# Taps' factors laid out channel by channel, and phases read across by ScalarE

## The chip, the cores and the metric

The kernel runs on one core of a Trainium2 chip. The metric is device time in microseconds, the median of several runs of the same kernel. The engines are TensorE (PE, with its weight loads shown as PEld), VectorE (DVE), ScalarE (ACT), GpSimd (POOL) and SyncE (SP, whose queue issues most DMAs). Each engine works through its own instructions in the order in which they were issued.

## The reference

Two branches over 2048 positions and 512 channels are mixed by a gate per position:

```python
dt = exp(log_dt)                                   # 512 channels
P  = exp(dt * (A_re + i A_im) * l)                 # channels x 128 states x 2048 positions
K  = einsum("dn,dnl,dn->dl", C, P, dt * B).real    # taps: 512 channels x 2048
a  = causal_convolution(u, K) + u * Dskip          # by FFT over 4096 points
b  = gelu(x @ w1 + b1) @ w2 + b2                   # 512 -> 1792 -> 512, x = u
g  = sigmoid((u * gate_w).sum(-1))
out = g * a + (1 - g) * b
```

## The kernel before

The work has two stages. The first, `front`, makes the taps K, runs the dense branch b, and does the first step of the signal's transform. The second, `conv`, finishes the convolution: second transform step of taps and signal, product, inverse transform, mix with the gate and output.

**The order.** `front` does not issue instructions as it goes. Its streams `dense`, `taps`, `signal` and `early` add tasks to a plan, each with an engine, a duration that the planner goes by (`mm(1.83, ...)`, `act(3.14, ...)`, for VectorE worked out from an element count by `vec`), a due time from the table `DUES`, and the tiles that it reads and writes. The planner plays the tasks through on paper and so fixes one order for every engine; the chip then follows that order. Work that waits on an engine holds up everything behind it on that engine.

**The taps.** The 512 channels are handled in 4 units of 128 (`prepare`, `coefficients`), each cut into 4 groups of `CW` = 32 channels, 16 groups in all. A position is split into a low part of 64 values and a high part of 32 values, so that a group's taps are, per channel, a product of two complex factors over the 128 states (the partitions): 32 high samples in `x` (tile `xc`, two copies in the space of `den`) and 64 low samples in `y` (one copy). Per group the steps are

- `phases` (VectorE, L703 and L695): integer phases `ph` by doubling, 33 samples x 32 channels, samples outside, channels inside.
- `waves` (ScalarE, L711 to L713): the absolute value, the sine and the cosine of the phases into `tt`, one copy in the space of `loft`.
- `begin` (ScalarE, L721): copies the first 4 samples of the high factor from `x4` into `xc`.
- `powers` (VectorE): three doublings from 4 to 32 samples by `cmul` (L594 to L597), which multiplies by a coefficient per channel from `zz`, through the scratch tiles `xt_` and `xv_`.
- `magnitudes` (GpSimd L740, VectorE L752 and five times L750): the 64 magnitudes `e`, which is `y[:, 1]`, by doubling from both ends.
- `rotate` (VectorE L763, L770, L774): turns magnitudes and sines into real and imaginary parts of `y`.
- `contract` (TensorE L788): for each channel, a matmul over the 128 states of the 32 high samples (weights, `x`) and the 64 low samples (moving, `y`), real and imaginary part, into one PSUM bank `pks`. Four channels at a time lie in the array's four column tiles. The trace shows two MATMULs for each fp32 product, so 128 for a group. VectorE then adds the skip term (L804), ScalarE copies the bank (L807), and after every second group the first transform step follows (`first_stage`, L489), whose results ScalarE copies (L815) and SyncE stores to `tk_d` in DRAM (L830) after each unit.

In the kernel before, all these tiles have the samples outside and the channels inside: one channel's samples lie 32 values (128 bytes) apart.

**The dense branch.** `hidden` (L985 to L987) multiplies in three parts of high and low halves into `ph` banks of PSUM, ScalarE applies the gelu (L1002) and casts the high half (L1005, `hh`), VectorE takes the difference (L1012, `hl`), and `output` (L1028 to L1031) multiplies by w2.

**The second stage.** `conv` begins with the taps reloaded from `tk_d` (tiles `tk` and `t`) and their transform (L1218), which is also where the chain of the first stage ends.

Of the kernel before, what the change touches and what calls it, by code (L numbers as in the profile page):

```python
# [17 lines left out]
P = 128  # L18
# [12 lines left out]
CW = 32  # L31
# [10 lines left out]
D_KA = 27.96  # L42
# [104 lines left out]
TWO_PI = 2.0 * PI  # L147
TURN = 2.0**32
# [201 lines left out]
def gated_mix(  # L350
# [18 lines left out]
    nc = tc.nc  # L369
# [33 lines left out]
    def front(pool, psum, keep, attic, loft, den, pr):  # L403

        pl = Plan()

        def tiles(n, shape, nm, dtype=F32, space=pool):
            return [space.tile(shape, dtype, name=f"{nm}{k}") for k in range(n)]

        def vec(n, fn, due, reads=(), writes=(), fast=1):  # L410

            return pl.add("DVE", 0.07 + n / 960.0 / fast, fn, due, reads, writes)

        def act(hold, fn, due, reads=(), writes=(), table=None):

            return pl.add("ACT", hold, fn, due, reads, writes, table)
# [20 lines left out]
        xc = [den[:, k : k + 4].rearrange("p k d -> p (k d)").rearrange("p (a b c) -> p a b c", a=2, c=CW) for k in (0, 4)]  # L437
        xt_, xv_ = (loft[:, k * 1024 : k * 1024 + 1024].rearrange("p (a b c) -> p a b c", a=2, c=CW) for k in range(2))
# [37 lines left out]
        step = [0]  # L476
# [108 lines left out]
            )  # L585
            vec(UW, lambda: v.tensor_copy(dtb, pus[1][:, 0:UW]), -190, [("pu", 1)], ["dtb"])

        def cmul(due, dst, a, br, bi, n, t, v, ka, kb, kd, kt, kv):

            w = a.shape[-1]  # L590
            br = br.unsqueeze(1).unsqueeze(1).to_broadcast([P, 2, n, w])
            bi = bi.unsqueeze(1).unsqueeze(1).to_broadcast([P, 2, n, w])
            vv, m = nc.vector, n * w
            vec(2 * m, lambda: vv.tensor_mul(t, a, br), due, [ka, *kb], [kt])  # L594
            vec(2 * m, lambda: vv.tensor_mul(v, a, bi), due, [ka, *kb], [kv])  # L595
            vec(m, lambda: vv.tensor_sub(dst[:, 0], t[:, 0], v[:, 1]), due, [kt, kv], [kd])
            vec(m, lambda: vv.tensor_add(dst[:, 1], t[:, 1], v[:, 0]), due, [kt, kv], [kd])  # L597
# [110 lines left out]

        def waves(t):
            def sines():  # L710
                nc.scalar.activation(tt[:, 0], ph, AF.Abs)  # L711
                nc.scalar.activation(tt[:, 1], ph, AF.Sin, scale=TWO_PI / TURN)
                nc.scalar.activation(tt[:, 0], tt[:, 0], AF.Sin, bias=half_pi, scale=-TWO_PI / TURN)  # L713

            act(3.14, sines, t + D_KA, ["ph"], ["tt"], "sin")

        def begin(c, k, t):

            cs = slice(c * CW, (c + 1) * CW)
            act(  # L720
                0.31, lambda: nc.scalar.copy(xc[k][:, :, 0:4], x4[:, :, :, cs]), t + D_KA,  # L721
                ["x4"], [("xc", k)],
            )
# [12 lines left out]

        def magnitudes(u, c, t):

            cs = slice(c * CW, (c + 1) * CW)
            pl.add("POOL", 0.1, lambda: nc.gpsimd.memset(e[:, 63], 1.0), t, [], ["y1"])  # L740

            def both(lo, step, n):

                a = e[:, lo : lo + n].copy()
                return bass.AP(a.tensor, a.offset, [a.ap[0], [step * CW, 2], *a.ap[1:]])

            def double(k):
                n = 1 << k
                an = ea[u % 2][:, k, cs].unsqueeze(1).unsqueeze(1).to_broadcast([P, 2, n, CW])
                nc.vector.tensor_mul(both(n, 64 - 3 * n, n), both(0, 64 - n, n), an)  # L750

            vec(CW, lambda: nc.vector.tensor_copy(e[:, 0], ea[u % 2][:, 5, cs]), t, [("ea", u % 2)], ["y1"])  # L752
            for k in range(5):
                vec(2 * CW << k, lambda k=k: double(k), t, [("ea", u % 2)], ["y1"])

        def rotate(t):

            v = nc.vector
            cc = tt[:, 0, 0:32]
            cc = bass.AP(cc.tensor, cc.offset, [cc.ap[0], [CW, 2], *cc.ap[1:]])  # L760

            def real():
                v.tensor_mul(  # L763
                    y[:, 0].rearrange("p (a b) c -> p a b c", a=2),
                    e.rearrange("p (a b) c -> p a b c", a=2),
                    cc,
                )
# [6 lines left out]
            vec(32 * CW, lambda: v.tensor_mul(e[:, 32:64], e[:, 32:64], tt[:, 1, 1:33]), t, ["tt"], ["y1"])  # L774

        pair = []

        def contract(u, c, k, t):
            g = u * NCH + c
            q = 0  # L780
            x = xc[k]

            def products(g0):
                for gg in range(g0, g0 + 4):
                    for r in range(2):
                        for j in range(4):
                            ch = j * 8 + gg
                            nc.tensor.matmul(  # L788
                                pks[q][32 * j : 32 * j + 32, :, gg],
                                x[:, r, :, ch],  # L790
                                y[:, r, :, ch],
                                start=(r == 0),
                                stop=(r == 1),
                                skip_group_check=True,
                            )
# [678 lines left out]
```

## Time and profile before

| what | value |
|---|---|
| median of 3 runs | 508.39 us (507.99 to 508.75) |
| span of the profiled execution | 505.5 us, 12181 instructions |
| TensorE clock granted, mean | 0.996 |
| busy over the span: PE, DVE, ACT, POOL | 495.2, 429.2, 365.0, 38.3 us |
| the sixteen contractions | L788, 2048 matmuls, the first at 71.6 us, the last at 376.3 us |

The profile carries the span of the profiled execution alone, from its first to its last instruction; the times of the runs take in what lies around it. In a row of instructions, the form on the right of an arrow is what is read, on the left what is written, as partitions x elements. "Busy" and "mean ns" follow, then the idle time of the engine in front of it with what ended it. In a row of a stretch of time stand its length and, for PE, PEld, DVE, ACT and POOL, the busy time with the number of instructions, then the granted TensorE clock, the share of the DMA engines, and GB/s. In a row of a waits view stand the total in us, the number of times, and the longest. In the timeline and the chain stand start and duration in us.

### The profile page before, as it was taken

The numbers are of one execution on the slowest core, as the hardware profiler recorded it, in microseconds if no ns is written. First come the engines' busy times: TensorE is split into PE (matmuls) and PEld (weight loads), VectorE is DVE, ScalarE is ACT, GpSimd is POOL, SyncE is SP. The second block draws the span as 40 slices with busy tenths as digits, with TensorE's granted clock in tenths as the row PEclk, the third lists the DMA queues.
The fourth block names the chain that finished last, engine by engine and source line by source line (L and its number), as shares of the span: only waits on it lengthen the run. The fifth ranks groups of instructions, "written<-read, shape, count | busy, mean of one in ns | idle before, by whom it ended". The sixth has DMA issues, their size and how long they took to land.

```text
span 505.5 us, 12181 instructions
## 1 busy us (share of the span) xinstructions
PE 495.2 (98%) x4802; PEld 379.0 (75%) x4802; DVE 429.2 (85%) x817; ACT 365.0 (72%) x632; POOL 38.3 (8%) x78
## 2 busy tenths in 40 slices
PE   8999999999999999999999999999999999999994
PEld 7898888898989889888988888998989522222551
DVE  4977999999999999999999999999940197877455
ACT  6999997899997789997767998636834465565310
POOL 2000000000000000001010020110100100231000
PEclk9999999999999999999999999999999999999998
DMA  8978686531858622855987244950477999989897
GB/s 286 350 280 278 188 243 213 161 126 43 280 138 246 200 73 72 254 168 116 232 217 241 75 64 128 186 100 3 154 219 169 259 389 389 338 305 391 294 344 299
DMA packets 81569, 107.56 MB, mean 213 GB/s; under 512 B 39284, under 2 KB 43784, under 8 KB 80968
## 3 DMA queue, kind: packets, MB, share of 16 engines
q1 hardware_dynamic: 74792, 82.80, 51.8%
q0 software_dynamic: 6016, 20.70, 15.4%
q10 hardware_dynamic: 704, 3.28, 1.8%
q8 instruction: 38, 0.62, 0.5%
q14 instruction: 19, 0.16, 0.1%
HBM read 61.14 MB, written 45.62 MB: 211 GB/s over the span
## 4 chain that ended last, share of the span: by engine, by line
PE 93%; DMA 2%; SPq 1%; DVE 1%; issue 1%; ACT 0%; POOL 0%; DVEq 0%; POOLq 0%
PE pk L788 12%; PE ph L985 10%; PE acc L1028 10%; PE ph L987 10%; PE ph L986 10%; PE acc L1029 9%; PE acc L1031 9%; PE p2k L1218 5%; PE p2u L1218 5%; PE pa L1257 3%; PE ph L489 3%; PE pb L1373 2%; DMA tk<-tk_d 1%; SPq L830 1%; DMA tk_d<-sk 1%; PE acc L1101 1%
## 5 line engine op out<-in xcount | busy, mean ns | idle before, releaser
L985 PE MATMUL ph<-xh,wh 128*128 128x256 f32 x448 | 127.5, 285 | 0.0
L987 PE MATMUL ph<-xh,wl 128*128 128x256 f32 x448 | 126.8, 283 | 0.0
L986 PE MATMUL ph<-xlo,wh 128*128 128x256 f32 x448 | 126.7, 283 | 0.0
L985 PEld LDWEIGHTS ph<-xh,wh 128*128 128x128 f32 x448 | 85.2, 190 | 6.9 <-issue 4.0
L986 PEld LDWEIGHTS ph<-xlo,wh 128*128 128x128 f32 x448 | 85.1, 190 | 2.1
L987 PEld LDWEIGHTS ph<-xh,wl 128*128 128x128 f32 x448 | 85.2, 190 | 0.0
L1028 PE MATMUL acc<-wh,hh 128*128 128x512 f32 x208 | 84.3, 405 | 0.0
L1029 PE MATMUL acc<-wl,hh 128*128 128x512 f32 x208 | 81.7, 393 | 0.0
L1031 PE MATMUL acc<-wh,hl 128*128 128x512 f32 x208 | 81.4, 391 | 0.0
L1002 ACT ACTIVATE ph<-ph,b1t 128x256 f32<-128x256 f32 x112 | 50.5, 451 | 25.0 <-PE ph L987 23.2
L788 PE MATMUL pk<-y,den 128*32 128x64 f32 x2048 | 61.4, 290 | 0.0
L788 PEld LDWEIGHTS pk<-y,den 128*32 128x32 f32 x2048 | 57.2, 136 | 2.6 <-issue 0.7
L1012 DVE TENSOR_TENSOR hl<-ph,hh 128x512 fp32r<-128x512 f32 (+1 forms) x62 | 38.2, 618 | 18.3 <-ACT hh L1005 10.8
L1028 PEld LDWEIGHTS acc<-wh,hh 128*128 128x128 f32 x208 | 39.1, 188 | 19.4 <-issue 8.8
L750 DVE TENSOR_TENSOR y<-y,ea 128x64 f32<-128x64 f32 (+4 forms) x80 | 45.3, 566 | 0.8 <-POOL y L740 0.3
L1031 PEld LDWEIGHTS acc<-wh,hl 128*128 128x128 f32 x208 | 39.1, 188 | 8.8
L1029 PEld LDWEIGHTS acc<-wl,hh 128*128 128x128 f32 x208 | 39.1, 188 | 6.1
L1226 ACT COPY k<-p2k 128x512 f32<-128x512 f32 x32 | 18.6, 586 | 27.2 <-issue 11.3
L594 DVE TENSOR_TENSOR loft<-den,zz 128x256 f32<-128x256 f32 (+2 forms) x48 | 37.2, 774 | 0.2
L595 DVE TENSOR_TENSOR loft<-den,zz 128x256 f32<-128x256 f32 (+2 forms) x48 | 37.2, 775 | 0.1
L763 DVE TENSOR_TENSOR y<-y,loft 128x2048 f32<-128x2048 f32 x16 | 36.6, 2286 | 0.4 <-ACT loft L713 0.2
L1005 ACT CAST hh<-ph 128x512 fp32r<-128x512 f32 (+1 forms) x62 | 33.0, 533 | 4.3 <-PE acc L1029 2.4
(197 smaller groups left out, 873.3 us busy)
## 6 DMA issues: line engine op xcount, KB each, us to landing
tk_d<-sk SPq DMA_DIRECT2D x32, 256.0 KB, 5.3
t_d<-sa SPq DMA_DIRECT2D x32, 256.0 KB, 5.1
tu_d<-attic SPq DMA_DIRECT2D x40, 128.0 KB, 3.5
attic<-in_xt_dram SPq DMA_DIRECT2D x16, 256.0 KB, 4.3
attic<-in_xs_dram SPq DMA_DIRECT2D x16, 256.0 KB, 5.0
xl_d<-xlo SPq DMA_DIRECT2D x8, 512.0 KB, 5.9
xh_d<-xh SPq DMA_DIRECT2D x8, 512.0 KB, 3.9
out_dram<-io SPq DMA_DIRECT2D x16, 256.0 KB, 3.1
```

The lines of the kernel that those rows point to most:

```text
L594: vec(2 * m, lambda: vv.tensor_mul(t, a, br), due, [ka, *kb], [kt])
L750: nc.vector.tensor_mul(both(n, 64 - 3 * n, n), both(0, 64 - n, n), an)
L788: nc.tensor.matmul(pks[q][32 * j : 32 * j + 32, :, gg], x[:, r, :, ch], y[:, r, :, ch], start=(r == 0), stop=(r == 1), skip_group_check=True,)
L985: nc.tensor.matmul(p, h, xh[xk][:, d], start=(d == 0), stop=False)
L986: nc.tensor.matmul(p, h, xlo[xk][:, d], start=False, stop=False)
L987: nc.tensor.matmul(p, lo, xh[xk][:, d], start=False, stop=(d == 3))
L1002: nc.scalar.activation(phs[q][:, n], phs[q][:, n], AF.Gelu_apprx_tanh, bias=b1t[:, f : f + 1])
L1012: nc.vector.tensor_sub(lo, phs[q][:, 0:nf], hi.bitcast(F32))
L1028: nc.tensor.matmul(a, h, wh[1][w], start=start, stop=False, skip_group_check=seeded)
L1029: nc.tensor.matmul(a, h, wl[1][w], start=False, stop=False, skip_group_check=seeded)
L1031: nc.tensor.matmul(a, l, wh[1][w], start=False, stop=stop, skip_group_check=seeded)
L1218: nc.tensor.matmul(out[64 * i : 64 * i + 64], w, x, start=True, stop=True)
```

## The change

All tiles of the two factors get channels outside and samples inside, so that one channel's samples are neighbours: `y` becomes `[P, 2, CW, 64]`, `xc` `[P, 2, CW, 32]`, `xt_` and `xv_` alike, `tt` `[P, 2, CW, 33]`. The phases `ph` stay as they were; the first two passes of `waves` read them across and write `tt` in the new order. `begin` reads `x4` across. `cmul` gets a form `inner`, in which the coefficient of a channel is repeated along the samples (the innermost dimension); `coefficients` keeps the old form. `magnitudes` and `rotate` do the same operations on the same counts in the new order. The matmuls of `contract` take `x[:, r, ch]` and `y[:, r, ch]`, 32 and 64 neighbours. The durations handed to the planner are unchanged.

```diff
-        y = pool.tile([P, 2, 64, CW], F32, name="y")
-        xc = [... .rearrange("p (a b c) -> p a b c", a=2, c=CW) for k in (0, 4)]
-        xt_, xv_ = (... .rearrange("p (a b c) -> p a b c", a=2, c=CW) for k in range(2))
-        tt = loft[:, 2048:4160].rearrange("p (a b c) -> p a b c", a=2, c=CW)
+        y = pool.tile([P, 2, CW, 64], F32, name="y")
+        xc = [... .rearrange("p (a c b) -> p a c b", a=2, c=CW) for k in (0, 4)]
+        xt_, xv_ = (... .rearrange("p (a c b) -> p a c b", a=2, c=CW) for k in range(2))
+        tt = loft[:, 2048:4160].rearrange("p (a c b) -> p a c b", a=2, c=CW)
...
-        def cmul(due, dst, a, br, bi, n, t, v, ka, kb, kd, kt, kv):
+        def cmul(due, dst, a, br, bi, n, t, v, ka, kb, kd, kt, kv, inner=False):
-            w = a.shape[-1]
-            br = br.unsqueeze(1).unsqueeze(1).to_broadcast([P, 2, n, w])
-            bi = bi.unsqueeze(1).unsqueeze(1).to_broadcast([P, 2, n, w])
+            w = CW if inner else a.shape[-1]
+            shape, at = ([P, 2, w, n], 3) if inner else ([P, 2, n, w], 1)
+            br = br.unsqueeze(1).unsqueeze(at).to_broadcast(shape)
+            bi = bi.unsqueeze(1).unsqueeze(at).to_broadcast(shape)
...
         def waves(t):
             def sines():
-                nc.scalar.activation(tt[:, 0], ph, AF.Abs)
-                nc.scalar.activation(tt[:, 1], ph, AF.Sin, scale=TWO_PI / TURN)
+                turned = ph.rearrange("p b c -> p c b")
+                nc.scalar.activation(tt[:, 0], turned, AF.Abs)
+                nc.scalar.activation(tt[:, 1], turned, AF.Sin, scale=TWO_PI / TURN)
                 nc.scalar.activation(tt[:, 0], tt[:, 0], AF.Sin, bias=half_pi, scale=-TWO_PI / TURN)
...
-                0.31, lambda: nc.scalar.copy(xc[k][:, :, 0:4], x4[:, :, :, cs]), t + D_KA,
+                0.31, lambda: nc.scalar.copy(xc[k][:, :, :, 0:4], x4[:, :, :, cs].rearrange("p a b c -> p a c b")), t + D_KA,
...
-                    t, x[:, :, n : 2 * n], x[:, :, 0:n], zz[:, 0, i, cs], zz[:, 1, i, cs], n,
-                    xt_[:, :, 0:n], xv_[:, :, 0:n], ("xc", k), ["zz"], ("xc", k), "xt", "xv",
+                    t, x[:, :, :, n : 2 * n], x[:, :, :, 0:n], zz[:, 0, i, cs], zz[:, 1, i, cs], n,
+                    xt_[:, :, :, 0:n], xv_[:, :, :, 0:n], ("xc", k), ["zz"], ("xc", k), "xt", "xv", True,
...
-            pl.add("POOL", 0.1, lambda: nc.gpsimd.memset(e[:, 63], 1.0), t, [], ["y1"])
+            pl.add("POOL", 0.1, lambda: nc.gpsimd.memset(e[:, :, 63], 1.0), t, [], ["y1"])
...
-                an = ea[u % 2][:, k, cs].unsqueeze(1).unsqueeze(1).to_broadcast([P, 2, n, CW])
+                an = ea[u % 2][:, k, cs].unsqueeze(1).unsqueeze(3).to_broadcast([P, 2, CW, n])
                 nc.vector.tensor_mul(both(n, 64 - 3 * n, n), both(0, 64 - n, n), an)
-            vec(CW, lambda: nc.vector.tensor_copy(e[:, 0], ea[u % 2][:, 5, cs]), t, ...)
+            vec(CW, lambda: nc.vector.tensor_copy(e[:, :, 0], ea[u % 2][:, 5, cs]), t, ...)
...
-                    y[:, 0].rearrange("p (a b) c -> p a b c", a=2),
-                    e.rearrange("p (a b) c -> p a b c", a=2),
+                    y[:, 0].rearrange("p c (a b) -> p a c b", a=2),
+                    e.rearrange("p c (a b) -> p a c b", a=2),
                     cc,
...
-                v.scalar_tensor_tensor(e[:, 0:32], e[:, 0:32], -1.0, tt[:, 1, 0:32], ALU.mult, ALU.mult)
+                v.scalar_tensor_tensor(e[:, :, 0:32], e[:, :, 0:32], -1.0, tt[:, 1, :, 0:32], ALU.mult, ALU.mult)
...
-                                x[:, r, :, ch],
-                                y[:, r, :, ch],
+                                x[:, r, ch],
+                                y[:, r, ch],
```

More of the change, by code (lines that the diff above doesn't have):

```diff
@@ L435, in front @@
         sk = pool.tile([P, 64, 2, 4, 8], F32, name="sk")
-        y = pool.tile([P, 2, 64, CW], F32, name="y")
-        xc = [den[:, k : k + 4].rearrange("p k d -> p (k d)").rearrange("p (a b c) -> p a b c", a=2, c=CW) for k in (0, 4)]
-        xt_, xv_ = (loft[:, k * 1024 : k * 1024 + 1024].rearrange("p (a b c) -> p a b c", a=2, c=CW) for k in range(2))
-        tt = loft[:, 2048:4160].rearrange("p (a b c) -> p a b c", a=2, c=CW)
+        y = pool.tile([P, 2, CW, 64], F32, name="y")
+        xc = [den[:, k : k + 4].rearrange("p k d -> p (k d)").rearrange("p (a c b) -> p a c b", a=2, c=CW) for k in (0, 4)]
+        xt_, xv_ = (loft[:, k * 1024 : k * 1024 + 1024].rearrange("p (a c b) -> p a c b", a=2, c=CW) for k in range(2))
+        tt = loft[:, 2048:4160].rearrange("p (a c b) -> p a c b", a=2, c=CW)
         ph = pool.tile([P, 33, CW], I32, name="phase")
@@ L739, in magnitudes @@
             cs = slice(c * CW, (c + 1) * CW)
-            pl.add("POOL", 0.1, lambda: nc.gpsimd.memset(e[:, 63], 1.0), t, [], ["y1"])
+            pl.add("POOL", 0.1, lambda: nc.gpsimd.memset(e[:, :, 63], 1.0), t, [], ["y1"])
             def both(lo, step, n):
-                a = e[:, lo : lo + n].copy()
-                return bass.AP(a.tensor, a.offset, [a.ap[0], [step * CW, 2], *a.ap[1:]])
+                a = e[:, :, lo : lo + n].copy()
+                return bass.AP(a.tensor, a.offset, [a.ap[0], [step, 2], *a.ap[1:]])
             def double(k):
                 n = 1 << k
-                an = ea[u % 2][:, k, cs].unsqueeze(1).unsqueeze(1).to_broadcast([P, 2, n, CW])
+                an = ea[u % 2][:, k, cs].unsqueeze(1).unsqueeze(3).to_broadcast([P, 2, CW, n])
                 nc.vector.tensor_mul(both(n, 64 - 3 * n, n), both(0, 64 - n, n), an)
-            vec(CW, lambda: nc.vector.tensor_copy(e[:, 0], ea[u % 2][:, 5, cs]), t, [("ea", u % 2)], ["y1"])
+            vec(CW, lambda: nc.vector.tensor_copy(e[:, :, 0], ea[u % 2][:, 5, cs]), t, [("ea", u % 2)], ["y1"])
             for k in range(5):
@@ L758, in rotate @@
             v = nc.vector
[L759 to L760 removed]
+            cc = tt[:, 0, :, 0:32]
+            cc = bass.AP(cc.tensor, cc.offset, [cc.ap[0], [1, 2], *cc.ap[1:]])
             def real():
                 v.tensor_mul(
[L764 to L765 removed]
+                    y[:, 0].rearrange("p c (a b) -> p a c b", a=2),
+                    e.rearrange("p c (a b) -> p a c b", a=2),
                     cc,
```

2 lines of the change are left out of this document (1 added, 1 removed).

## The prediction, made before the changed kernel ran

> **What bounds the kernel now.** I read the page's busy times and the chain that ended last first, then the engines' busy times stretch by stretch, then the waits, and last the timeline around one channel group.
>
> ```profile
> PE 495.2 (98%) x4802; PEld 379.0 (75%) x4802; DVE 429.2 (85%) x817; ACT 365.0 (72%) x632; POOL 38.3 (8%) x78
> PE 93%; DMA 2%; SPq 1%; DVE 1%; issue 1%; ACT 0%; POOL 0%; DVEq 0%; POOLq 0%
> ```
>
> These two lines say that TensorE is the bound and that whatever shortens it is won. The stretches say something else:
>
> ```profile
> 20.00:50.00 30.00, 30.00 (x195) 27.39 (x195) 24.33 (x61) 29.47 (x57) 0.23 (x2) 1.00 0.88 303
> 50.00:370.50 320.50, 320.47 (x3712) 277.82 (x3711) 313.81 (x599) 265.92 (x445) 22.10 (x45) 1.00 0.57 158
> 370.50:402.40 31.90, 30.86 (x313) 25.38 (x311) 5.10 (x10) 12.60 (x26) 1.91 (x3) 1.00 0.80 198
> ```
>
> After the times stand the busy times of PE, PEld, DVE, ACT and POOL. From 50 to 370.5 us, where the taps are made, TensorE is busy 320.47 of 320.5 us and VectorE 313.81. Two engines are full. TensorE's work can shrink as far as it likes: the stretch keeps at least VectorE's 313.8 us, so 6.7 us are to be had there. What VectorE waited for between 20 and 371 us is little:
>
> ```profile
> DVE hl L1012 <- ACT hh L1005: 4.0, 7, 1.3
> DVE pk L804 <- PE pk L788: 2.5, 6, 0.6
> ```
>
> From 370.5 us the end of the taps leads on without slack: the last rotation on VectorE, the last contraction, its evacuations, the store of the taps to DRAM, their reload, the transform.
>
> ```profile
> 369.29 1.22 DVE L774 TENSOR_TENSOR y<-y,loft 128x1024 f32<-128x1024 f32 x1
> 372.81 3.76 PE pk L788 x127
> 391.38 5.04 DMA tk_d<-sk
> 402.36 2.49 PE p2k L1218 x8
> ```
>
> TensorE's dense work queued behind the last contraction fills the same time (30.86 of 31.9 us), so both legs start with that contraction. From 402.4 us on nothing changes. The end of the kernel therefore moves with the end of VectorE's last rotation, 370.5 us.
>
> **The change part by part.** Instructions, tiles, DMAs, queues and the order on each engine stay as they are: the durations that the planner goes by are the old ones. What changes is which address each element has.
>
> *Contraction (TensorE).* Per group 128 matmuls of 64 columns, four column tiles at a time, so 32 rounds.
>
> ```profile
> 71.61 3.84 PE L788 MATMUL pk<-y,den 128*32 128x64 f32 x128
> 75.38 0.50 PE L1028 MATMUL acc<-wh,hh 128*128 128x512 f32 x1
> 411.64 1.03 PE L1218 MATMUL p2k<-tk,cc 128*64 128x512 f32 x4
> 412.50 1.03 PE L1218 MATMUL p2k<-tk,f 128*64 128x512 f32 x4
> L788 PEld LDWEIGHTS pk<-y,den 128*32 128x32 f32 x2048 | 57.2, 136 | 2.6 <-issue 0.7
> L1028 PEld LDWEIGHTS acc<-wh,hh 128*128 128x128 f32 x208 | 39.1, 188 | 19.4 <-issue 8.8
> L1218 PEld LDWEIGHTS p2k<-t,cc 128*64 128x64 f32 x32 | 2.3, 137 | 4.6 <-ACT sa L1269 2.3 <-issue 2.3
> ```
>
> From 71.61 to the next work at 75.38 are 3.77 us, or 118 ns a round: 1.84 ns a column, with a step of 128 bytes from one to the next. The transform's fp32 matmuls read neighbours: two rounds in 0.86 us, 512 columns each, 0.84 ns a column. Weights tell the same: 64 more neighbouring columns cost 51 ns (188 against 137), so 32 columns should load 25 ns faster than 64; the 32 strided ones take 136, as long as 64. So I take 2.2 times as a step's price. Side by side, a round is 64 x 0.84 = 54 ns, with a little for handover 60, and the weights' 26 ns hide under it. A contraction falls from 3.77 to 1.92 us, 1.85 less; sixteen give 29.6. Ends: 2.05 a contraction (54 ns), or nothing if the round isn't set by the step. But only what lies on VectorE's path counts: its waits for the contraction (2.5), the last contraction's own 1.85, and the 2.2 us (370.51 to 372.81) by which TensorE was late for it. Gain: 6.6 us.
>
> Where the next limit of such short matmuls lies is a second question. The row: eight matmuls in eight tiles start within 40 ns,
>
> ```profile
> 59.37 0.64 PE L489 MATMUL ph<-attic,c1t 32*64 32x512 f32 x1
> 59.41 0.64 PE L489 MATMUL pu<-ux,c1t 32*64 32x512 f32 x1
> ```
>
> the first and the last of eight, some 6 ns apart, so four need 24 ns of the 60. [...]
>
> *Phases and first powers (ScalarE).* The first two passes of the sines now read the phases across: 33 x 32 values, each 128 bytes from the next. They are written side by side, and the third pass is as before. The copy that starts the powers reads 256 values across.
>
> ```profile
> L711 ACT ACTIVATE loft<-phase 128x1056 f32<-128x1056 int32 x16 | 17.5, 1093 | 0.0
> L712 ACT ACTIVATE loft<-phase 128x1056 f32<-128x1056 int32 x16 | 17.5, 1094 | 0.2
> L643 ACT ACTIVATE ea<-pr 128x128 f32<-128x128 f32 x24 | 5.3, 298 | 0.0
> L721 ACT COPY den<-x 128x256 f32<-128x256 f32 x16 | 6.2, 407 | 11.5 <-PE pk L788 8.1 <-DVE x L597 3.4
> ```
>
> ScalarE has no strided read in this trace. Neighbours cost (1093 - 298) / 928 = 0.86 ns a column. Nearest is TensorE's read with the very same step, 1.0 ns dearer a column: 1056 columns, 1.0 us a pass after rounding down. The ends are nothing and 1.06. A gain is excluded, since no fewer values are read. That is 2.0 us a wave and 0.25 for the copy, 36 us over sixteen groups. In 50 to 370.5 us ScalarE has 54.6 us free, so it would fit on average. [...]
>
> It doesn't fit in place. A wave can't start before the rotation ahead has read the sines' only tile (or the phases are doubled). Behind it on ScalarE's queue stand a table load, the gelu and the cast whose difference VectorE takes next; behind that, in order, stands all of VectorE.
>
> ```profile
> 104.78 1.22 DVE L774 TENSOR_TENSOR y<-y,loft 128x1024 f32<-128x1024 f32 x1
> 106.30 1.09 ACT L711 ACTIVATE loft<-phase 128x1056 f32<-128x1056 int32 x1
> 107.41 1.28 ACT L712 ACT_TABLE_LOAD   x1
> 108.70 1.10 ACT L712 ACTIVATE loft<-phase 128x1056 f32<-128x1056 int32 x1
> 109.70 1.18 ACT L713 ACTIVATE loft<-loft,half_pi 128x1056 f32<-128x1056 f32 x1
> 110.90 1.28 ACT L1002 ACT_TABLE_LOAD   x1
> 112.20 0.93 ACT L1002 ACTIVATE ph<-ph,b1t 128x256 f32<-128x256 f32 x2
> 113.16 0.59 ACT L1005 CAST hh<-ph 128x512 fp32r<-128x512 f32 x1
> 113.78 0.69 DVE L1012 TENSOR_TENSOR hl<-ph,hh 128x512 fp32r<-128x512 f32 x1
> ```
>
> The rotation ends at 106.00, the wave starts at 106.30 and ScalarE runs without a gap to 113.75; VectorE takes the result at 113.78. Two more microseconds in the wave are two on VectorE, and they are not won back. The timeline has nine places where the slack behind a wave is under 1.5 us; the first and the last:
>
> ```profile
> 50.54 1.17 ACT L713 ACTIVATE loft<-loft,half_pi 128x1056 f32<-128x1056 f32 x1
> 51.88 2.28 DVE L763 TENSOR_TENSOR y<-y,loft 128x2048 f32<-128x2048 f32 x1
> 346.97 0.39 ACT L721 COPY den<-x 128x256 f32<-128x256 f32 x1
> 347.84 0.42 DVE L594 TENSOR_TENSOR loft<-den,zz 128x256 f32<-128x256 f32 x1
> ```
>
> Lateness less slack at the nine gives 15.7 us, some fourteen smaller ones another 5. Against that, TensorE is no longer late for ScalarE, which lets a few waves and gelus start earlier. I take 15, ends 8 and 25.
>
> *VectorE.* The same instructions over the same counts, now in runs of 4 to 32 neighbours, with the coefficient read again and again along a run.
>
> ```profile
> L750 DVE TENSOR_TENSOR y<-y,ea 128x64 f32<-128x64 f32 x16 | 3.5, 220 | 0.5 <-POOL y L740 0.3
> L594 DVE TENSOR_TENSOR loft<-den,zz 128x1024 f32<-128x1024 f32 x16 | 19.5, 1221 | 0.1
> ```
>
> Only the first doubling (64 values) and the 32-value copy ahead of it go to single values; at the price of a step that is 0.1 us a group. Rows of 33 in the sines begin on odd words half of the time, which I put at one value more for each of 64 rows. Together 2 us. The repeated coefficient (1792 x 2 in the powers, 1984 in the doublings, sixteen times: 89,000 values) I cost at nothing, since the address stays in place; the other end is the step's 1.0 ns, 89 us. GpSimd's fill of 32 values becomes strided, hidden behind the copy that VectorE does then; uncovered it would be 32 ns a group at the step's price.
>
> **The sum.** Span 505.5 - 6.6 + 2 + 15 = 515.9 us. The profile gives no time of its own beside the span; the median of the runs, 508.39, is 2.9 above it. 515.9 + 2.9 = 518.8, 2% slower.
>
> **The rivals.**
> *ScalarE reads across for nothing* (ends faster). The place is the two passes at L711 and L712; at price nothing there are no new stalls: 505.5 - 6.6 + 2 + 2.9 = 503.8. It decides as long as the stalls stay under 4.6 us, about 0.4 us a pass. For it: it is another engine with its own reader. Against: both reads of TensorE pay for the step. [...] Chance 0.17; a price near that point, thus no change, 0.07.
> *The contraction isn't bound by the step* (the change does not do what it says), by a floor on starts, say. The 1.85 us at the end are lost, the waits for TensorE are covered by VectorE's own lateness: 520.7. For it: 128 short matmuls in a row are seen nowhere else. Against: the weights' 136 ns. [...] Chance 0.09.
> *VectorE pays for the repeated coefficient.* 518.8 + up to 89 us; already at a tenth it is 528. Nothing in the trace shows such an operand. Chance 0.06.
> *TensorE alone is the bound* and all 29.6 us come through: 478.8. VectorE's 313.81 of 320.5 excludes nearly all of it. Chance 0.02.
>
> **How the numbers follow.** My forecast has 0.59. A difference under 0.2%, 1.0 us, can't be told from none. Slower: 0.59 + 0.09 + 0.06 = 0.74; faster 0.17 + 0.02 = 0.19; same 0.07. The likeliest case's own range, with stalls of 8 to 25, is 511.8 to 528.8. The range reaches down to the rival without a price, 504, and up to 532 for a tenth of the coefficient's price.
>
> **What would show it.** Matmuls at L788: a contraction near 1.9 us. L711 and L712 near 2.1 us, L713 unchanged. VectorE's waits for ScalarE (hh, the sines) at 10 us or more, its waits for the contraction gone, TensorE's busy time in the taps some 30 us lower, with idle in front of L788 and L1028. VectorE's L594, L750 and L763 within 10% of before. The prediction is wrong if L711 stays at 1.1 us, or if VectorE's stalls behind slower passes stay under 5 us.

## The result, and the profile after

| kernel | median (lowest to highest) | ratio to before | span of the profiled execution |
|---|---|---|---|
| before, same chip | 508.19 us (507.72 to 508.75) | 1 | |
| after | 527.94 us (527.1 to 528.63) | 1.040, interval 1.0378 to 1.0423 | 526.7 us |

The change makes the kernel 4.0% slower, 19.75 us. The forecast was 518.8 us, 504 to 532: the sign is right, the time lies in the range, and the loss is about twice the 10.4 us forecast.

The span grew by 21.2 us (505.5 to 526.7). The busy times and the shares of the chain that ended last, from the page of the kernel after:

```profile
PE 483.9 (92%) x4802; PEld 355.2 (67%) x4802; DVE 431.1 (82%) x817; ACT 402.2 (76%) x632; POOL 38.7 (7%) x78
PE 43%; ACT 35%; DVE 13%; issue 5%; DMA 2%; SPq 1%; POOL 0%; DVEq 0%; ACTq 0%; POOLq 0%
```

Before, TensorE held 93% of the chain and ScalarE nothing. Now ScalarE holds 35% of it, although it is busy for only 76% of the span. The engines' busy times by stretch, cut where VectorE's last rotation ends (370.5 us before, 393.7 us now):

```profile
50.00:393.70 343.70, 310.73 (x3725) 256.92 (x3724) 316.03 (x601) 303.14 (x446) 22.73 (x45) 0.98 0.54 148
393.70:426.00 32.30, 31.31 (x308) 23.11 (x308) 5.15 (x11) 13.28 (x27) 1.71 (x2) 1.00 0.84 212
```

The third busy time is VectorE's. It did the same work in the taps, 316.03 us instead of 313.81, but the stretch is 23.2 us longer: 27.7 us idle instead of 6.7. TensorE now has 33.0 us idle in it. What VectorE waited for in this stretch (total, times, longest):

```profile
DVE hl L1014 <- ACT hh L1007: 9.3, 10, 2.4
DVE phase L704 <- ACT loft L714: 7.4, 8, 1.4
DVE y L765 <- ACT loft L715: 4.1, 3, 2.3
DVE xlo L891 <- ACT xh L889: 1.9, 1, 1.9
DVE loft L596 <- ACT den L723: 1.1, 1, 1.1
DVE wl L891 <- ACT wh L889: 1.1, 3, 0.6
DVE loft L649 <- ACT loft L637: 0.6, 1, 0.6
```

All of it is ScalarE, 25.5 us in all against 1.6 in the same stretch before; the contraction's evacuation (L804 before) is gone from the list. The groups of instructions behind it, shapes kept apart (busy, mean ns, idle in front); the lines of before moved by one to three:

```profile
L713 ACT ACTIVATE loft<-phase 128x1056 f32<-128x1056 int32 x16 | 35.0, 2187 | 1.0 <-DVE phase L696 1.0
L714 ACT ACTIVATE loft<-phase 128x1056 f32<-128x1056 int32 x16 | 35.0, 2187 | 0.2
L715 ACT ACTIVATE loft<-loft,half_pi 128x1056 f32<-128x1056 f32 x16 | 18.7, 1170 | 0.0
L790 PE MATMUL pk<-y,den 128*32 128x64 f32 x2048 | 32.8, 220 | 3.8 <-DVE y L776 2.1 <-ACT attic L507 1.5
L595 DVE TENSOR_TENSOR loft<-den,zz 128x1024 f32<-128x1024 f32 x16 | 19.6, 1224 | 0.1
L765 DVE TENSOR_TENSOR y<-y,loft 128x2048 f32<-128x2048 f32 x16 | 36.7, 2292 | 4.3 <-ACT loft L715 4.1
L752 DVE TENSOR_TENSOR y<-y,ea 128x64 f32<-128x64 f32 x16 | 4.4, 274 | 0.3
```

ScalarE's two passes take 2187 ns each instead of 1093, 35.0 us more over sixteen groups; the third pass reads its own output in order and didn't change (1170 ns; before, as L713, 1169). The contractions take 32.8 us in all on TensorE; before it was 61.4:

```profile
L788 PE MATMUL pk<-y,den 128*32 128x64 f32 x2048 | 61.4, 290 | 0.0
```

VectorE's products with a repeated coefficient are as fast as ever (L595, 1224 ns; before, as L594, 1221). One wave in the timeline of the kernel after (start, duration), the same kind of place that the prediction showed for before:

```profile
111.67 2.19 ACT L713 ACTIVATE loft<-phase 128x1056 f32<-128x1056 int32 x1
113.89 1.28 ACT L714 ACT_TABLE_LOAD   x1
115.18 2.13 ACT L714 ACTIVATE loft<-phase 128x1056 f32<-128x1056 int32 x1
117.22 1.16 ACT L715 ACTIVATE loft<-loft,half_pi 128x1056 f32<-128x1056 f32 x1
118.40 1.28 ACT L1004 ACT_TABLE_LOAD   x1
119.69 0.93 ACT L1004 ACTIVATE ph<-ph,b1t 128x256 f32<-128x256 f32 x2
120.66 0.59 ACT L1007 CAST hh<-ph 128x512 fp32r<-128x512 f32 x1
121.28 0.69 DVE L1014 TENSOR_TENSOR hl<-ph,hh 128x512 fp32r<-128x512 f32 x1 [1.36 <-ACT hh L1007]
```

From the first pass to the handover are 9.6 us; before they were 7.45 (106.30 to 113.75). For 1.36 us of the 2.1 us more VectorE stands idle: it waits for the cast before it can make `hl`, and all of its own work is queued behind.

At the end of the taps the chain is shorter, but less than forecast. The timeline there, then a piece of the chain that ended last:

```profile
392.52 1.22 DVE L776 TENSOR_TENSOR y<-y,loft 128x1024 f32<-128x1024 f32 x1
394.45 1.99 PE L790 MATMUL pk<-y,den 128*32 128x64 f32 x128
```

```profile
395.52 0.60 ACT hh L1007
396.14 0.70 DVE hl L1014
396.89 0.39 PE ph L987
398.57 0.57 PE ph L489 x2
...
423.26 0.85 PE p2k L1220 x2
```

The last contraction ends 2.7 us after the rotation instead of 6.1 (376.57 less 370.51): 3.4 won. But the chain no longer goes through the taps' store and reload. It goes through TensorE's dense work, which waits 0.44 us for a late `hl` (until L987 at 396.89) and stands another 0.52 us ahead of L489 at 400.10, and the transform of the taps starts 26.8 us after the contraction instead of 25.8. The other leg is hardly shorter: the wait of the transform's weights for the reload (`tk`) ends at 422.98, 0.3 us earlier. With 0.3 us further on, 1.3 of the 3.4 are given back: 2.0 remain. So the span is 23.2 longer before this point and 2.0 shorter behind it.

### The profile page after: what moved, and what is told of

Read it like the earlier page. It is cut to its first block, busy times and chain, and to the rows that moved or that the text cites. A ratio compares the mean times of both kernels' runs of the same rounds, so it can differ in the third digit from the quotient of the medians.

```text
span 526.7 us, 12185 instructions
## 1 busy us (share of the span) xinstructions
PE 483.9 (92%) x4802; PEld 355.2 (67%) x4802; DVE 431.1 (82%) x817; ACT 402.2 (76%) x632; POOL 38.7 (7%) x78
## 4 chain that ended last, share of the span: by engine, by line
PE 43%; ACT 35%; DVE 13%; issue 5%; DMA 2%; SPq 1%; POOL 0%; DVEq 0%; ACTq 0%; POOLq 0%
PE p2u L1220 6%; PE p2k L1220 5%; ACT loft L713 5%; PE ph L987 5%; ACT loft L714 5%; PE ph L988 4%; PE ph L989 4%; ACT ph L1004 4%; PE pa L1259 3%; ACT L1004 3%; PE acc L1033 3%; PE acc L1030 3%; PE acc L1031 3%; ACT loft L715 2%; ACT L714 2%
## 5 line engine op out<-in xcount | busy, mean ns | idle before, releaser
L987 PE MATMUL ph<-xh,wh 128*128 128x256 f32 x448 | 129.2, 288 | 10.7 <-ACT sk L817 4.3
L987 PEld LDWEIGHTS ph<-xh,wh 128*128 128x128 f32 x448 | 86.2, 192 | 20.5 <-ACT sk L817 5.6
L1030 PE MATMUL acc<-wh,hh 128*128 128x512 f32 x208 | 85.6, 412 | 8.7 <-ACT hh L1007 5.4
L1033 PE MATMUL acc<-wh,hl 128*128 128x512 f32 x208 | 83.6, 402 | 4.3 <-DVE hl L1014 4.1
L988 PEld LDWEIGHTS ph<-xlo,wh 128*128 128x128 f32 x448 | 86.2, 192 | 1.9
L1014 DVE TENSOR_TENSOR hl<-ph,hh 128x512 fp32r<-128x512 f32 (+1 forms) x62 | 38.4, 621 | 26.8 <-ACT hh L1007 17.3
L752 DVE TENSOR_TENSOR y<-y,ea 128x64 f32<-128x64 f32 (+4 forms) x80 | 46.3, 579 | 0.6
L765 DVE TENSOR_TENSOR y<-y,loft 128x2048 f32<-128x2048 f32 x16 | 36.7, 2292 | 4.3 <-ACT loft L715 4.1
L1228 ACT COPY k<-p2k 128x512 f32<-128x512 f32 x32 | 18.7, 586 | 26.4 <-issue 11.3
L595 DVE TENSOR_TENSOR loft<-den,zz 128x256 f32<-128x256 f32 (+2 forms) x48 | 37.4, 779 | 0.3
L790 PE MATMUL pk<-y,den 128*32 128x64 f32 x2048 | 32.8, 220 | 3.8 <-DVE y L776 2.1
L713 ACT ACTIVATE loft<-phase 128x1056 f32<-128x1056 int32 x16 | 35.0, 2187 | 1.0 <-DVE phase L696 1.0
```

The lines of the kernel that those rows point to most:

```text
L713: nc.scalar.activation(tt[:, 0], turned, AF.Abs)
L987: nc.tensor.matmul(p, h, xh[xk][:, d], start=(d == 0), stop=False)
L988: nc.tensor.matmul(p, h, xlo[xk][:, d], start=False, stop=False)
L1014: nc.vector.tensor_sub(lo, phs[q][:, 0:nf], hi.bitcast(F32))
L1030: nc.tensor.matmul(a, h, wh[1][w], start=start, stop=False, skip_group_check=seeded)
L1033: nc.tensor.matmul(a, l, wh[1][w], start=False, stop=stop, skip_group_check=seeded)
```

## The experiments

Theory: ScalarE pays about 1.1 us for each pass that reads values one by one 128 bytes apart, its chain of wave, table load, gelu and cast has next to no slack, and the lateness becomes idle time of a VectorE that has no room to make it up. Rivals: VectorE's new forms or the contraction's new form carry the loss; the new wait for the phases (L704) is a loss of its own; TensorE's relief counts in full.

**1. The new layout without the turned reads** (`waves_in_order`).

```
-                turned = ph.rearrange("p b c -> p c b")
+                turned = ph.rearrange("p b c -> p (b c)").rearrange("p (c b) -> p c b", c=CW)
```

> The changed kernel, but ScalarE's two passes read the phases in the order in which they lie, one neighbour after the other (the values are then those of other samples). Theory, that the step in ScalarE's reads makes the whole loss by stalls on VectorE: the passes fall from 2.19 to about 1.09 us, VectorE's waits for hh, for the sines and for the phases from 25 us back to 5 at most, last rotation ends near 369 us, time 502 to 507 us. Rival, that VectorE's new order or the contraction loses time: 520 us or more stay.

Measured: 501.55 us, ratio 0.9869 (0.9834 to 0.9904), just under the range of the theory. Its passes and its stretch of the taps:

```profile
L713 ACT ACTIVATE loft<-phase 128x1056 f32<-128x1056 int32 x16 | 17.4, 1090 | 2.0 <-DVE phase L696 2.0
50.00:370.00 320.00, 304.14 (x3860) 255.69 (x3859) 315.09 (x601) 270.69 (x449) 22.74 (x45) 1.00 0.58 162
```

One line of address arithmetic is worth 26.4 us (527.94 less 501.55). Everything else in the change, VectorE's forms included, is a gain of 1.3%.

**2. The turned reads alone** (`waves_across_alone`), in the kernel before.

```
-                nc.scalar.activation(tt[:, 0], ph, AF.Abs)
-                nc.scalar.activation(tt[:, 1], ph, AF.Sin, scale=TWO_PI / TURN)
+                turned = ph.rearrange("p b c -> p c b")
+                into = [tt[:, k].rearrange("p b c -> p (b c)").rearrange("p (c b) -> p c b", c=CW) for k in range(2)]
+                nc.scalar.activation(into[0], turned, AF.Abs)
+                nc.scalar.activation(into[1], turned, AF.Sin, scale=TWO_PI / TURN)
```

> The kernel before with nothing but ScalarE's two passes reading the phases across (the values are those of other samples); the contraction keeps its steps. Theory: the passes cost 2.19 us, VectorE stalls as in the changed kernel, and the 1.85 us of the last contraction and some 2 of VectorE's new forms cancel: 526 to 534 us. Rival, that TensorE's relief mattered within the taps: well above 534. Rival, that the new layout on VectorE makes a good part of the loss: below 520.

Measured: 530.99 us, 1.0449 (1.0407 to 1.0492). VectorE's three largest waits in the taps are those of the kernel after:

```profile
DVE hl L1014 <- ACT hh L1007: 10.8, 10, 2.6
DVE phase L703 <- ACT loft L714: 9.6, 9, 1.5
DVE y L765 <- ACT loft L715: 4.1, 3, 2.4
```

So the loss needs nothing of the new layout.

**3. The quick contraction alone** (`contraction_alone`), in the kernel before.

```
-            x = xc[k]
+            x = xc[k].rearrange("p a b c -> p a (b c)").rearrange("p a (c b) -> p a c b", c=CW)
+            yy = y.rearrange("p a b c -> p a (b c)").rearrange("p a (c b) -> p a c b", c=CW)
...
-                                x[:, r, :, ch],
-                                y[:, r, :, ch],
+                                x[:, r, ch],
+                                yy[:, r, ch],
```

> The kernel before with nothing but the matmuls of the contraction reading 32 and 64 neighbours (values of other samples). Theory, that VectorE is the second bound: a contraction falls from 3.77 to about 1.9 us, TensorE's busy time by 28 us, yet the time only by VectorE's waits and the end of the chain, 6.6 us: 500 to 504 us. Rival, that TensorE alone binds: 479 us.

Measured: 499.58 us, 0.984 (0.9801 to 0.9879), just under the 500 to 504 expected.

```profile
L789 PE MATMUL pk<-y,den 128*32 128x64 f32 x2048 | 33.0, 220 | 1.0 <-DVE y L774 1.0
50.00:370.00 320.00, 305.42 (x3869) 257.52 (x3869) 314.67 (x604) 267.89 (x450) 22.27 (x45) 1.00 0.58 163
```

TensorE's contractions are 28 us shorter and the kernel 9.0 us. VectorE is busy for 314.67 of 320 us: there is the wall. The gains don't add, though. From the turned reads alone (ratio 1.0449) to the whole change (1.040) the new layout is worth some 2.5 us, with intervals that overlap a little, so it may be less. A VectorE that is late for ScalarE covers most of what a quick contraction saves.

**4. One pass across** (`one_pass_across`): the kernel after, with the first pass in order and the second as it is.

```
-                nc.scalar.activation(tt[:, 0], turned, AF.Abs)
+                nc.scalar.activation(tt[:, 0], ph.rearrange("p b c -> p (b c)").rearrange("p (c b) -> p c b", c=CW), AF.Abs)
```

> The changed kernel, but of the two passes only the sine reads across, the absolute value reads neighbours (values of other samples). Theory: a wave is 1.1 us dearer instead of 2.2; where the slack behind a wave is 0.03 to 0.5 us most of it still stalls VectorE, so some 9 to 12 us of the loss stay: 511 to 518 us. If stalls had a threshold near a whole wave's price, it would be back at 505; if the first pass made none of them, at 526.

Measured: 511.4 us, 1.0068 (1.0043 to 1.0093). From no pass across to one it is 9.9 us, from one to two 16.5. Per group that is 0.62 and 1.03 us for 1.09 us of ScalarE each time: the first microsecond still finds slack, the second almost none.

One thing else differs between these two kernels. TensorE's granted clock is 1.00 throughout the taps before and, from 50 to 370 us, with one pass across, but in the kernel after it is 0.51 in four stretches of 3.5 us (from 61.2, 143.1, 190.9 and 218.2 us), hence the mean of 0.98. VectorE is busy all through these four, 14.00 of 14.00 us, so it doesn't stall there. Whether a part of its later waits comes from them, no run separates.

**5. What a read costs.** Three kernels, timed once each; what is read from them are the durations of passes and matmuls. `read_patterns`: the kernel after, where the first pass reads pairs of neighbours with jumps of 128 bytes, the second steps by 8 bytes, and the contraction's moving operand is pairs with jumps of 256 bytes.

```
+                pairs = ph.rearrange("p b (c two) -> p c b two", two=2)
+                skip = flat.rearrange("p (n two) -> p two n", two=2)
...
+            yy = y.rearrange("p a c b -> p a (c b)").rearrange("p a (b c two) -> p a c b two", c=CW, two=2)
```

> The changed kernel with other orders of the reads alone (values of other samples): the first pass reads the phases in pairs of neighbours with a jump of 128 bytes after each pair, the second pass every second value (step 8 bytes), the contraction's moving operand pairs of neighbours, its weights neighbours as in the changed kernel. Theory, that a read needs two neighbouring 4-byte values to run at full rate: first pass 1.1 us, second 2.2 us, contraction 1.9 to 2.0 us. Rival, that each jump costs about a nanosecond: first pass 1.6 us, contraction near 2.9 us. Rival, that what counts is two values within 16 bytes: second pass 1.1 us.

`read_steps`: the first pass steps by 16 bytes, the second by 12, the moving operand by 128; the weights stay side by side.

```
+                four = flat.rearrange("p (n k) -> p k n", k=4)
+                three = flat.rearrange("p (n k) -> p k n", k=3)
...
+            yy = y.rearrange("p a c b -> p a (c b)").rearrange("p a (b c) -> p a b c", c=CW)
```

> The changed kernel with other steps of the reads (values of other samples): first pass every fourth value (step 16 bytes), second pass every third (step 12 bytes); the contraction's moving operand 128 bytes apart again, its weights neighbours. Theory, that a value pays when it is the only one taken from its 16 bytes: first pass 2.2 us, second pass between 1.2 and 1.7 us; contraction 3.7 us, matmul 290 ns with a weight load of 110. Rival, that only long jumps pay: both passes 1.1 to 1.3 us. Time without a second rival 515 to 525 us.

`weights_across`: the kernel after with only the weights 128 bytes apart.

```
-            x = xc[k]
+            x = xc[k].rearrange("p a c b -> p a (c b)").rearrange("p a (b c) -> p a b c", c=CW)
```

> The changed kernel, but the contraction's weights (32 values) are read 128 bytes apart (values of other samples), the moving operand neighbours as in the changed kernel. Theory, that the moving operand sets a round and the weights load under it: weight load back to about 136 ns, a contraction at 1.95 to 2.1 us, time as the changed kernel's 526 to 530 us. Rival, that the weights set it: 3 us or more a contraction.

Measured: 504.13, 522.73 and 525.26 us, the last just under the 526 to 530 expected. The groups of the first:

```profile
L715 ACT ACTIVATE loft<-phase 128x1056 f32<-128x1056 int32 x16 | 19.8, 1236 | 1.9 <-DVE phase L696 1.9
L716 ACT ACTIVATE loft<-phase 128x1056 f32<-128x1056 int32 x16 | 19.2, 1198 | 0.2
L793 PE MATMUL pk<-y,den 128*32 128x64 f32 x2048 | 33.4, 219 | 1.1 <-DVE y L778 1.1
```

of the second:

```profile
L715 ACT ACTIVATE loft<-phase 128x1056 f32<-128x1056 int32 x16 | 35.4, 2211 | 0.7 <-DVE phase L696 0.7
L716 ACT ACTIVATE loft<-phase 128x1056 f32<-128x1056 int32 x16 | 27.1, 1692 | 0.2
L793 PE MATMUL pk<-y,den 128*32 128x64 f32 x2048 | 60.5, 289 | 2.1 <-ACT attic L507 1.4 <-DVE y L778 0.8
```

and of the third:

```profile
L790 PE MATMUL pk<-y,den 128*32 128x64 f32 x2048 | 35.1, 224 | 3.9 <-DVE y L776 2.0 <-ACT attic L507 1.7
L790 PEld LDWEIGHTS pk<-y,den 128*32 128x32 f32 x2048 | 32.4, 141 | 7.0 <-issue 2.8 <-ACT attic L507 2.2
```

For ScalarE's pass of 1056 values: neighbours 1.09 us, a step of 8 bytes 1.20, pairs with jumps 1.24, a step of 12 bytes 1.69, of 16 bytes 2.21, of 128 bytes 2.19. The theory put down for the first run, that only neighbours are read at full rate, fell at the second pass (2.2 us expected, 1.20 measured), and so did the rival by which every jump costs. In these six patterns the time goes with how many values are taken from the same 16 bytes: two cost little more than neighbours (1.20 and 1.24 us), one costs double, whether the next lies 16 or 128 bytes on (2.21 and 2.19 us). At a step of 12 bytes half of the values are alone in their 16 bytes, which by an estimate halfway between 1.09 and 2.19 would give 1.64 us; 1.69 were measured. A value that is alone costs 1.0 ns more here (1.10 us over 1056 values). TensorE follows suit: its moving operand sets the round (33.4 us in pairs, 60.5 apart), and weights apart cost 2.3 us in all.

**6. Is the wait for the phases a loss of its own?** Eight waits, 7.4 us: VectorE wants to overwrite the only tile of phases while ScalarE's second pass still reads it. Two kernels free the tile after the first pass, by a cast of the phases across into `tt`, after which everything reads in order. They issue one pass more per wave. `cast_first`:

```
+                nc.scalar.copy(tt[:, 1], turned)
+                nc.scalar.activation(tt[:, 0], tt[:, 1], AF.Abs)
+                nc.scalar.activation(tt[:, 1], tt[:, 1], AF.Sin, scale=TWO_PI / TURN)
```

> The changed kernel with four passes in place of three: one reads the phases across and only writes them as float, side by side; the absolute value and the sine then read neighbours. ScalarE's time for a wave stays (2.19 + 1.1 + 1.1 + 1.17 in place of 2 x 2.19 + 1.17 us), but the phases' only tile is free after the first pass, some 3.5 us earlier. Theory, that a part of the loss is VectorE waiting to overwrite the phases (7.4 us): 520 to 525 us. Rival, that only ScalarE's time counts: 527 us or more.

Measured: 534.2 us, 1.0516 (1.0494 to 1.0538), a miss. The waits for the phases were gone, but the cast writes where the rotation before still reads the sines, so it started later than the first pass had to:

```profile
L713 ACT CAST loft<-phase 128x1056 f32<-128x1056 int32 x16 | 34.9, 2181 | 4.7 <-DVE y L777 3.7 <-DVE phase L696 1.0
```

`cast_into_cosine` writes the cast into the cosines' half instead, which the rotation has left by then:

```
+                nc.scalar.copy(tt[:, 0], turned)
+                nc.scalar.activation(tt[:, 1], tt[:, 0], AF.Sin, scale=TWO_PI / TURN)
+                nc.scalar.activation(tt[:, 0], tt[:, 0], AF.Abs)
```

> As cast_first, but the pass across writes where the first pass of the changed kernel writes, so that it starts as early as there, and not after the rotation's last operation; the sine is then made from it, the absolute value in place. ScalarE's time for a wave as in the changed kernel. Theory, that VectorE's wait for the phases (7.4 us) is a loss of its own: 519 to 523 us. Rival, that a stall taken away at the phases comes back at the next result that VectorE takes from ScalarE: 525 to 529 us.

Measured: 530.75 us, 1.0449 (1.0401 to 1.0498), not faster than the kernel after (1.0378 to 1.0423) and a little above the rival's range. VectorE's two largest waits in the taps:

```profile
DVE hl L1015 <- ACT hh L1008: 16.6, 11, 3.3
DVE y L766 <- ACT loft L716: 6.8, 3, 2.5
```

No wait for the phases, and 7.3 and 2.7 us more in the two others. It is the same idle time under another name. Around one wave the kernel after shows

```profile
139.46 0.19 DVE L704 CUSTOM_DVE_ANT_0 phase<-phase,ti 128x64 uint16<-128x64 uint16 x1 [1.41 <-ACT loft L714]
142.67 0.42 DVE L1014 TENSOR_TENSOR hl<-ph,hh 128x256 fp32r<-128x256 f32 x1 [1.17 <-ACT hh L1007]
```

and this kernel shows

```profile
143.82 0.42 DVE L1015 TENSOR_TENSOR hl<-ph,hh 128x256 fp32r<-128x256 f32 x1 [3.01 <-ACT hh L1008]
```

1.41 + 1.17 = 2.58 against 3.01. VectorE meets ScalarE's lateness once; where it has been stopped at the phases, it is stopped for less at the cast. The theory that this wait was a loss of its own fell. The extra 2.8 us over the kernel after would fit the wave itself: four passes that hang on each other take about 0.17 us longer than the three of the kernel after (6.83 against 6.66 us from the start to the handover), sixteen times 2.7 us. But the two intervals overlap, so the extra time isn't certain. Two tiles for the phases, which would take the wait away without a longer wave, weren't tried.

**7. The new layout in a few groups only.** Where the slack behind a wave is large, the quick contraction should be free. `groups_10_15` has the new layout in groups 10 and 15, `groups_2_10_13_15` in two more; all others work as before, in the same tiles.

```
+        NEW = (10, 15)
...
+                                x[:, r, ch] if new else xo[k][:, r, :, ch],
+                                y[:, r, ch] if new else yo[:, r, :, ch],
...
+        def pick(new, old, g):
+            return new if g in NEW else old
```

> The new layout for the groups 10 and 15 alone, the old one for the other fourteen. Theory: behind the waves of these two the changed kernel shows hardly a stall (0.3 us), so their price is small, while the last contraction's 1.85 us, what is left of TensorE's lateness for it and the wait at group 10 are won: 503 to 506 us. Rival, that slack is used up wherever a wave is longer: 507 us or more.

> The same for four groups. Theory: TensorE is relieved of 7.4 us instead of 3.7, which helps little, and the two waves more may stall 0.5 us each: 503 to 507 us. Rival as before: 508 us or more.

Measured: 506.14 us, 0.9967 (0.995 to 0.9984), and 506.35 us, 0.9971 (0.9953 to 0.9988). Both are 0.3% quicker than before, the first just above the range expected of it. The second is no better: VectorE now waits 1.7 us for the phases, which it doesn't in the first. So places with enough slack seem to be few.

**8. Halves in pairs** (`halves_paired`). In experiment 5 TensorE's contractions took 33.4 us in pairs against 32.8 side by side, and ScalarE's pass at a step of 8 bytes 1.20 us against 1.09. So only `y` is laid out anew, with sample s and sample s + 32 of a channel as neighbours. Phases, sines and the high factor keep their old layout, and ScalarE reads everything in order.

```
-        y = pool.tile([P, 2, 64, CW], F32, name="y")
+        y = pool.tile([P, 2, 32, CW, 2], F32, name="y")
...
-                a = e[:, lo : lo + n].copy()
-                return bass.AP(a.tensor, a.offset, [a.ap[0], [step * CW, 2], *a.ap[1:]])
+                a = e[:, lo : lo + n, :, 0].copy()
+                return bass.AP(a.tensor, a.offset, [a.ap[0], [(hi - 32 - lo) * 2 * CW + 1, 2], *a.ap[1:]])
...
+            cc = cc.unsqueeze(3).to_broadcast([P, 32, CW, 2])
...
+                v.tensor_mul(y[:, 0], e, cc)
...
-                                pks[q][32 * j : 32 * j + 32, :, gg],
+                                pks[q][32 * j : 32 * j + 32, :, gg].rearrange("p (h b) -> p b h", h=2),
```

> The kernel before with one tile laid out anew: in y, sample s and sample s + 32 of a channel are neighbours (32 x 32 channels x 2), and phases, sines, powers and the high factor stay as they were, so ScalarE's three passes stay at 1.09, 1.09 and 1.16 us. The contraction's moving operand reads pairs with jumps of 256 bytes (by the earlier runs as fast as neighbours, 1.95 us a contraction; with weights 128 bytes apart 2.07) and writes its columns to PSUM in the order 0, 32, 1, 33, and so on. VectorE's rotation into the real part reads each cosine twice running; the doublings of the magnitudes (1984 values a group) and the two halves of the rotation into the imaginary part (2048) now step by 8 bytes. My theory (an engine pays for values that stand alone in 16 bytes, and pairs cost little): VectorE's step of 8 bytes costs nothing or what ScalarE's did, 0.1 ns a value, 0 to 6.4 us over sixteen groups; with the 8.6 us that the quick contraction gained by itself 499 to 506 us, doubling of 1024 values 1.22 to 1.33 us. Rival (VectorE pays for any step, as its first doubling did at 256 bytes, 0.84 ns a value): 54 us more, over 540 us, doubling of 1024 values 2.1 us.

Measured: 500.23 us (498.6 to 502.13), ratio 0.9837 (0.9811 to 0.9864).

```profile
L750 DVE TENSOR_TENSOR y<-y,ea 128x1024 f32<-128x1024 f32 x16 | 19.5, 1220 | 0.1
L763 DVE TENSOR_TENSOR y<-y,loft 128x2048 f32<-128x2048 f32 x16 | 36.6, 2285 | 0.4 <-ACT loft L713 0.2
L784 PE MATMUL pk<-y,den 128*32 128x64 f32 x2048 | 39.5, 231 | 0.6 <-DVE y L770 0.5
```

The doubling of 1024 values before:

```profile
L750 DVE TENSOR_TENSOR y<-y,ea 128x1024 f32<-128x1024 f32 x16 | 19.5, 1219 | 0.1
```

VectorE pays nothing for its step of 8 bytes. A contraction takes about 2.4 us, more than the 2.07 that pairs with weights apart led one to expect; its columns also go to PSUM in another order, but what the rest is, the runs don't tell. It costs nothing, since TensorE isn't the bound any more: the kernel is as fast as that of experiment 3, leaves nothing of the computation out, and takes 5.2% less than the kernel after.

## Why the prediction was right and wrong

**The bound: right.** VectorE filled the taps' stretch. With the contraction 28 us shorter, the kernel gains 9.0 us and not 29.6 (experiment 3); that TensorE alone binds, at 478.8, is refuted.

**The contraction: right.** 1.99 us in the row above, 32.8 in all, forecast 1.92 and 30.7; 128 matmuls in 1.99 us start 15.5 ns apart on average. So the rival by which the contraction keeps its 3.77 us, by a floor on starts, say, is refuted.

**ScalarE's passes: right in kind, 9% low.** 1.09 us a pass dearer, forecast 1.0, just above the end of 1.06; the copy that starts the powers went from 407 to 655 ns, as forecast. That TensorE's price for a step would hold on ScalarE was the choice that set the sign. It was carried over from one engine to another without a row of ScalarE's to show it; in experiment 5 pairs cost both little (ScalarE 1.24 us a pass against 1.09, TensorE 33.4 us for all contractions against 32.8) and single values both much (2.19 and 60.5 us). The rival by which ScalarE reads for nothing (503.8) is refuted by the rows, and 501.55 in experiment 1 shows what it would have given.

**VectorE: right in kind, the size by luck.** VectorE is busy 2.2 us more in the taps, forecast 2 (the two items named there add up to some 2.5). Of these, no run shows the price put on the rows of 33: the rotation's operations, which read them, went from 2286, 1220 and 1219 ns to 2292, 1224 and 1223, but L595, which reads none, went from 1221 to 1224 as well. But over the whole span it is busy for 427.7 us in experiment 3, with the old forms, for 428.9 in experiment 1, with the new ones, and for 431.1 in the kernel after: the new forms cost 1.2 us, and the other 2.2 go with the turned reads. The first doubling takes 274 ns instead of 220, the repeated coefficient nothing. That last rules out a rival which the time alone would leave: 527.94 us is also what a tenth of the coefficient's price would give (528).

**The stalls: the term that was sized too low.** Forecast 15 us (8 to 25). VectorE's idle time in the taps grew by 21.0, and 2.5 us of waits for the contraction went, so the new stalls are 23.5 us; undoing the reads saves 26.4 us of time. The prediction had 20.7 over the places (15.7 + 5) and took off 5.7, because waves and gelus would start earlier with TensorE not late. Experiment 2 has the same passes and no relief of TensorE: VectorE waits 28.7 us for ScalarE there, 25.5 in the kernel after and 1.6 before. So the places cost some 27 us without any relief (22.6 would be 20.7 with passes 9% dearer), and the relief took off some 3, and not 5.7; how much is uncertain by about 2 us, since the profile of experiment 2 is that of the slowest of its four runs (533.14 us, median 530.99). The sum over the places was too low and the deduction too large. Which places the sum missed isn't worked out. Experiment 4 shows the shape: the first pass costs 0.62 us of its 1.09, the second 1.03.

**The gain of 6.6: too high in this company.** The waits for the contraction, 2.5, went. Of the 4.05 at the end of the taps 2.0 came through: the contraction came out as forecast, TensorE was 0.7 us late for it instead of 2.3 (the 2.2 of the prediction), and then both legs behind it took longer, and the dense one, which the prediction had as filling the same time, became the longer by 0.3 us. With the stalls gone the gain is there in full: experiment 1 is 7.0 us below its own runs of before (508.6).

**What would show it.** The waits for ScalarE and the missing waits for the contraction came as said, and L595, L752's largest form and L765 stayed within 1%. TensorE's busy time in the taps fell by 9.7 us, not by 30. Part of that is its granted clock: four times 3.5 us at 0.51 make some 7 us, by estimate. What the rest is, is open. The wait for the phases (L704), 7.4 us, stood nowhere in the prediction. It followed from the same late second pass, and experiment 6 finds no gain in taking it away.

## What to carry to other kernels

Before a cost is moved to an engine that has time to spare on average, read the slack behind each moved operation in that engine's queue: 55 us of free ScalarE couldn't hide 35 us of longer passes, because a full VectorE waited in order behind them. When two engines are full, relieving one is worth little beyond what the other leaves idle (28 us off TensorE brought 9.0 in experiment 3), and less still if the relief itself makes the other wait (beside the turned reads it brought some 2.5 us, perhaps less). And when a reader wants neighbours, ask whether pairs are enough: pairing two halves of a tile gave the kernel nearly all of the gain (500.2 us against 499.6 in experiment 3) with nothing to pay on ScalarE or VectorE.

## What was not expected of the hardware

A step of 8 bytes costs ScalarE 10% and a step of 12 bytes 55% (1.20 and 1.69 us against 1.09), but a step of 16 bytes costs as much as one of 128 (2.21 and 2.19 us). VectorE's products at a step of 8 bytes take as long as at neighbours (1220 against 1219 ns for 1024 values), and so do those with an operand that is read again and again (1224 against 1221). TensorE's moving operand read in pairs 256 bytes apart is as fast as neighbours (33.4 against 32.8 us for all contractions). And TensorE's granted clock, 1.00 throughout the taps before, was 0.51 in four stretches of 3.5 us in the kernel after, where TensorE stands idle for 33.0 us in all; no run here shows why.
